# Down products of the second layer: from twenty-four tile products to seven block products

## The chip, the cores and the metric

The kernel runs on one core of one Trainium2 chip. The metric is the device time of one execution in microseconds (us). "TensorE" is the matrix engine (PE in the profile), "VectorE" is DVE, "ScalarE" is ACT, "GpSimd" is POOL; SP only issues DMAs here.

## The reference, cut to what matters

A chunked attention (2 batches, 8 heads, 768 positions, head size 64) gives 1536 tokens of 512 features. Two layers follow, of which only these lines matter:

```python
for e in range(4):                                   # first layer: w1[e] 512x1024, w2[e] 1024x512
    out += p[:, e:e+1] * (np.maximum(x @ w1[e], 0) @ w2[e])
h = x @ w_in                                         # second layer: w_in 512x2048
g = np.where(h > 0, h, np.exp(np.minimum(h, 0)) - 1)
return g @ w_out                                     # w_out 2048x512
```

## The kernel before, in words

**Precision.** Every operand of a product is split into a high and a low part ("hh" and "hl" for the hidden values, "uh"/"ul" and "dh"/"dl" for up and down weights, "xh"/"xl" for the layer's input): a cast on ScalarE makes the high part and a subtraction on VectorE or GpSimd the low one (`split_task`, L245). A product is three matmuls: high by high, low by high, high by low.

**Units.** Both layers are cut into units (u, g): u counts slices of 512 hidden features (8 in the first layer, 4 in the second), g is one of two groups of 768 tokens. `SEQ` lists the 24 units in order; the last eight, from (8, 0) to (11, 1), are the second layer. A unit is one `up` and then one `down`.

**up (L552)** is a Strassen form (Winograd's): hidden features, input features and tokens are each halved, and 7 block products replace 8. `ORDER` is 1, 7, 6, 2, 5, 4, 3; each product comes in two column halves j, so there are 14 steps of 6 matmuls of 128x384. Three pairs of PSUM banks take part: `ba` (products 1 and 2), `bh` (7 and 4), `bb` (6, 5, 3). ScalarE copies product 1 into `bb`, and products 7 and 6 aside into SBUF (`keep`, L580) before the next product accumulates on the same bank; VectorE adds (`plus`, L589). In the second layer each 128x384 result goes through ELU in `activate` (L497): two activations on ScalarE (L522, L523), one operation on VectorE (L528), and then a cast (L533) and a subtraction (L243) that make hh and hl.

**down (L640)** takes six blocks of 128 tokens, each 12 matmuls of 128x512 (4 slices of features by 3) into one bank of a ring of six, 72 matmuls in all, and adds the bank to y in SBUF: ScalarE copies it at u = 8 (L693), VectorE adds at u = 9 to 11 (L695). At u = 11 y goes to DRAM (L697); the last block is done in two halves of 256 columns. y of both groups stays in SBUF.

**Weights.** Up weights come as four blocks per j into `rawp`; `prep_pair` (L283) splits three of them, makes four block sums on GpSimd (L300), and splits those. Down weights of a unit come into `rawd` and are split by `prep_down` (L307). The second layer's weights arrive as 64-bit floats; `convert` (L321) turns them to 32 bits during the first layer and stores them in a DRAM stash.

**Between the layers** the first layer's y is transposed on TensorE by blocks (`flip`, L699), and `combine` (L434) makes the sums of the new input's blocks (4 differences and 4 splits of 128x768) on VectorE or GpSimd as `RANK["engx1"]` says.

**Order.** Nothing is issued in program order. `Plan` collects tasks with an engine, a duration and a rank, and `issue` simulates the engines and issues, on whichever engine can start first, the ready task of least rank. So each engine's queue order is fixed when the kernel is built, and an engine waits at the head of its queue. The offsets in `RANK` and the engines in `BY` are constants.

Of the kernel before, what the change touches and what calls it, by code (L numbers as in the profile page):

```python
# [19 lines left out]
P = 128  # L20
# [4 lines left out]
NB = S // P  # L25
# [20 lines left out]
Q = 2 * P  # L46

# [16 lines left out]
    "probs": 23.52, "a0": 2.68, "a0s": 1.6, "lead": 7.03, "pair": 7.15, "pairs": -2.83, "plead": 4.25, "c0": -100.24,  # L64
# [22 lines left out]


def pick(key, default):
    return BY.get(key, default)  # L90


ORDER = (1, 7, 6, 2, 5, 4, 3)

PLAIN = ((4, 5, 6, 7), (4, 5, 6, 7))


class Plan:

# [77 lines left out]
def kernel(ctx, tc, att, w1, w2, w_in, w_out, probs, out):  # L177
# [374 lines left out]
    def up(u, g, rank):  # L552
# [3 lines left out]
        for n, (p, j) in enumerate([(p, j) for j in range(2) for p in ORDER] if apart else [(p, j) for p in ORDER for j in range(2)]):  # L556
# [54 lines left out]
            elif p == 3:  # L611
                act(j, 1, acc, kb)
# [385 lines left out]
```

## Time and profile before

| | |
|---|---|
| median of 3 runs | 809.6 us (809.51 to 810.88) |
| span of the profiled execution | 808.4 us |
| TensorE busy | 797.4 us (99%) |
| VectorE / ScalarE / GpSimd busy | 513.0 / 422.9 / 264.2 us (63% / 52% / 33%) |
| granted TensorE clock | 0.999 |
| DMA | 72.11 MB, 89 GB/s over the span |

The profiled execution has a span of 808.4 us from its first to its last instruction; its own time outside the profiler is not listed, and the median of the three runs is 1.2 us above that span. Matmul durations overlap, because matmuls are pipelined; the spacing of their starts is what they cost.

### The profile page before, as it was taken

What the parts mean: (1) busy time and instruction counts of PE and PEld (TensorE: products, weight loads), DVE (VectorE), ACT (ScalarE), POOL (GpSimd) and SP (SyncE); (2) the same over time, 40 slices, a digit from 0 to 9 for tenths busy, and PEclk for the clock granted to TensorE, in tenths of its full rate; (3) what the DMA queues carried; (4) which work ended last, traced back from release to release, by engine and by line L of the source; (5) the groups of instructions that cost most, each with busy time, mean ns of one, the idle gap of its engine ahead of it and who ended that gap; (6) DMA issues with size and microseconds to landing.
All of it is one profiled execution on the core that took longest, in us unless ns stands there. A gap on an engine that the chain in (4) does not pass through costs nothing.

```text
span 808.4 us, 12197 instructions
## 1 busy us (share of the span) xinstructions
PE 797.4 (99%) x4684; PEld 720.5 (89%) x4684; DVE 513.0 (63%) x860; ACT 422.9 (52%) x869; POOL 264.2 (33%) x250
## 2 busy tenths in 40 slices
PE   7999999999999999999999999999999999999998
PEld 6888889989989989989989889899898898898997
DVE  5895559985865875865875745745734536537533
ACT  6877635715425425425435336456766555555642
POOL 2447374305124124223322422653214215205202
PEclk9999999999999999999999999999999999999999
DMA  8965013522511511511421300213003003000112
GB/s 313 344 245 170 29 52 118 182 92 68 172 61 66 194 61 59 208 53 67 156 78 66 131 1 1 70 46 94 1 1 105 0 1 105 1 1 1 38 41 78
DMA packets 27418, 72.11 MB, mean 89 GB/s; under 512 B 3168, under 2 KB 3424, under 8 KB 27360
## 3 DMA queue, kind: packets, MB, share of 16 engines
q1 hardware_dynamic: 27360, 71.34, 26.0%
q8 instruction: 36, 0.59, 0.3%
q14 instruction: 22, 0.18, 0.1%
HBM read 59.79 MB, written 11.53 MB: 88 GB/s over the span
## 4 chain that ended last, share of the span: by engine, by line
PE 90%; DVE 3%; ACT 3%; DMA 2%; POOL 1%; issue 1%; SPq 0%; ACTq 0%; DVEq 0%; POOLq 0%
PE bank L662 47%; PE bank L568 39%; DMA qk<-in_att_dram 2%; PE bank L628 1%; DMA area<-in_w_in_dram 1%; POOL rawp L300 1%; PE bank L784 1%; PE bank L861 1%; PE bank L707 1%; ACT e L812 0%; DVE abd L849 0%; ACT abd L849 0%; PE bank L841 0%; DVE ul L243 0%; DVE m L806 0%
## 5 line engine op out<-in xcount | busy, mean ns | idle before, releaser
L662 PE MATMUL bank<-dh,hh 128*128 128x512 f32 x580 | 225.8, 389 | 0.0
L662 PE MATMUL bank<-dh,hl 128*128 128x512 f32 x580 | 225.2, 388 | 0.0
L662 PE MATMUL bank<-dl,hh 128*128 128x512 f32 x580 | 225.1, 388 | 0.0
L568 PE MATMUL bank<-xh,uh 128*128 128x384 f32 x644 | 218.4, 339 | 0.9 <-DVE c L589 0.5
L568 PE MATMUL bank<-xh,ul 128*128 128x384 f32 x644 | 216.8, 337 | 0.0
L568 PE MATMUL bank<-xl,uh 128*128 128x384 f32 x644 | 216.7, 337 | 0.0
L243 POOL TENSOR_TENSOR hl<-c,hh 128x384 fp32r<-128x384 f32 x63 | 69.6, 1117 | 224.8 <-ACT hh L533 221.1
L662 PEld LDWEIGHTS bank<-dh,hl 128*128 128x128 f32 x580 | 108.9, 188 | 23.1 <-DVE hl L508 0.2
L662 PEld LDWEIGHTS bank<-dl,hh 128*128 128x128 f32 x580 | 108.9, 188 | 21.3
L662 PEld LDWEIGHTS bank<-dh,hh 128*128 128x128 f32 x580 | 108.9, 188 | 21.1
L568 PEld LDWEIGHTS bank<-xh,uh 128*128 128x128 f32 x644 | 120.9, 188 | 3.2 <-DVE c L589 1.1
L568 PEld LDWEIGHTS bank<-xl,uh 128*128 128x128 f32 x644 | 120.9, 188 | 0.8
L568 PEld LDWEIGHTS bank<-xh,ul 128*128 128x128 f32 x644 | 120.9, 188 | 0.1
L300 POOL TENSOR_TENSOR rawp<-rawp 128x256 f32<-128x256 f32 x96 | 86.2, 910 | 20.6 <-DVE ul L243 14.4
L688 DVE SCALAR_TENSOR_TENSOR y<-bank,pr,y 128x512 f32<-128x512 f32 x84 | 62.6, 746 | 41.2 <-PE bank L662 41.1
L243 POOL TENSOR_TENSOR hl<-area,hh 128x384 fp32r<-128x384 f32 x32 | 36.7, 1161 | 152.8 <-ACT hh L533 152.1
L243 DVE TENSOR_TENSOR ul<-rawp,uh 128x512 fp32r<-128x512 f32 (+1 forms) x71 | 67.7, 969 | 28.5 <-ACT uh L247 28.4
L247 ACT CAST uh<-rawp 128x512 fp32r<-128x512 f32 (+1 forms) x76 | 51.9, 685 | 60.9 <-POOL rawp L300 59.5
L375 ACT ACTIVATE area<-area 128x512 f32<-128x512 f32 x32 | 20.3, 634 | 82.8 <-DVE area L366 82.7
L528 DVE SCALAR_TENSOR_TENSOR area<-area,bank 128x384 f32<-128x384 f32 x32 | 17.6, 549 | 68.7 <-ACT area L523 68.7
L580 ACT COPY bank<-bank 128x384 f32<-128x384 f32 x46 | 21.2, 463 | 73.7 <-PE bank L568 73.7
L243 POOL TENSOR_TENSOR dl<-rawd,dh 128x512 fp32r<-128x512 f32 x14 | 22.5, 1611 | 66.4 <-ACT dh L247 66.4
(87 smaller groups left out, 953.4 us busy)
## 6 DMA issues: line engine op xcount, KB each, us to landing
rawp<-in_w_dram SPq DMA_DIRECT2D x18, 512.0 KB, 3.3
rawd<-in_w_dram SPq DMA_DIRECT2D x36, 256.0 KB, 3.8
qk<-in_att_dram SPq DMA_DIRECT2D x11, 768.0 KB, 6.3
area<-in_w_in_dram SPq DMA_DIRECT2D x16, 512.0 KB, 3.7
stash<-area SPq DMA_DIRECT2D x32, 256.0 KB, 2.2
area<-in_w_out_dram SPq DMA_DIRECT2D x16, 512.0 KB, 3.7
v<-in_att_dram SPq DMA_DIRECT2D x12, 512.0 KB, 5.3
rawp<-stash SPq DMA_DIRECT2D x16, 256.0 KB, 2.7
```

What stands on the lines that cost most here:

```text
L243: e.tensor_tensor(out=dst, in0=a, in1=b, op=ALU.subtract)
L247: add("A", t_a(n), rank, lambda: A.copy(out=hi(), in_=src), rkeys, hkeys)
L300: lambda o=o, a=a, b=b, op=op: G.tensor_tensor(out=r[:, o], in0=r[:, a], in1=r[:, b], op=op),
L375: lambda: A.activation(out=t, in_=t, func=AF.Copy, scale=2.0**-20, bias=1.0),
L528: lambda: V.scalar_tensor_tensor(out=r, in0=r, scalar=-1.0, in1=v, op0=ALU.add, op1=ALU.max),
L568: PE.matmul(out=acc, lhsT=s[:, k], rhs=x[g][ib][:, k], start=(first and k == 0 and m == 0), stop=(k == 1 and m == 2), skip_group_check=True,)
L580: add("A", t_a(TN), r - 2, lambda: A.copy(out=dst, in_=acc), kb, kd)
L628: PE.matmul(out=acc, lhsT=s[:, k], rhs=x[0][ib][:, k], start=(q == 0 and k == 0 and m == 0), stop=(q == 1 and k == 1 and m == 2),)
L662: PE.matmul(out=po, lhsT=s[f][half][:, t0 : t0 + P], rhs=w[f][:, c], start=(q == 0 and i == 0), stop=(q == NF - 1 and i == 2),)
L688: lambda: V.scalar_tensor_tensor(out=yy(), in0=po, scalar=p, in1=yy(), op0=ALU.mult, op1=ALU.add),
L707: PE.transpose(ft[:, kt], y[g][tb][:, kt * P : (kt + 1) * P], ident)
L784: PE.matmul(out=s4[64 * cp : 64 * cp + 64, hp, ch], lhsT=qbd[:, hp, c], rhs=k[:, hp, c], start=True, stop=True,)
```

## The change

1. The second layer's down product becomes the same seven block products as up: output features, hidden features and tokens halved, the down weights stationary, the hidden values moving (`down2`). It comes out transposed (features on the partitions, tokens along the free axis), and the output in DRAM has that layout; the host turns it round.
2. The hidden values are kept unsplit in "quads" of 128x768. `hidden_diff` makes four differences on VectorE per unit, `hidden_split` seven splits (ScalarE casts; four subtractions on VectorE and three on GpSimd) into four rotating buffers `sh`/`sl`. The eight casts and eight subtractions of 128x384 in `activate` go.
3. The down weights need block sums too. They are made on GpSimd during the first layer (`sums_ahead`, at the places in `ROUNDS`), stored to DRAM and loaded by `prep_pair(kind="d")`; `prep_down` is no longer used in the second layer.
4. The second layer's order is up(8,0), up(8,1), down(8,0), up(9,0), down(8,1), ..., down(11,0), down(11,1). Up and down take turns on the bank pairs: `bh` stays with every run, the other three pairs rotate (`turn_banks`).
5. y of the second layer has one buffer for both groups. After each down it is stored to DRAM in four pieces of 384 KB, and loaded back before the same group's next down. `gather` adds the products to it, in twelve operations of 128x384 per unit (on ScalarE the first six of those at u = 8).
6. Memory: dh/dl, rawd and y become single tiles that the second layer reuses once the first has ended (`switch2`); y of the second group is freed for low parts of the down weights ("late").
7. Ranks change: `pp` 40.18 to 16.59, `fx` -18.99 to 2.61, `x1` 51.82 to 47.43, `engx1` "GGVV" to "VVVV", and new ones for the added tasks. `up` is unchanged but for where its results go.

```diff
+ROUNDS = {6: [(NU1, "d")], 10: [(NU1 + 1, "d")], 12: [(NU1 + 2, "d")], 14: [(NU1 + 3, "d")]}
+SUMS = {s for ss in ROUNDS.values() for s in ss}
...
-    rawd = [t(f"rawd{f}", [CH]) for f in range(NF)]
-    dhi = [t(f"dh{f}", [CH], F32R) for f in range(NF)]
-    dlo = [t(f"dl{f}", [CH], F32R) for f in range(NF)]
-    hh = [[t(f"hh{f}_{n}", [TN], F32R) for n in range(2)] for f in range(NF)]
-    hl = [[t(f"hl{f}_{n}", [TN], F32R) for n in range(2)] for f in range(NF)]
-    y = [[t(f"y0_{tb}", [DM]) for tb in range(NB)]]
+    dmem = t("dmem", [2 * NF * CH], F32R)
+    dhi, dlo = ([dmem[:, (n * NF + f) * CH : (n * NF + f + 1) * CH] for f in range(NF)] for n in range(2))
+    rmem = t("rmem", [NF * CH])
+    rawd = [rmem[:, f * CH : (f + 1) * CH] for f in range(NF)]
+    sh = [t(f"sh{s}", [2, TN], F32R) for s in range(4)]
+    sl = [t(f"sl{s}", [2, TN], F32R) for s in range(4)]
+    hh = [[sh[2 * n + f // 2][:, f % 2] for n in range(2)] for f in range(NF)]
+    hl = [[sl[2 * n + f // 2][:, f % 2] for n in range(2)] for f in range(NF)]
+    ymem = [t("y0", [NB * DM])]
+    y = [[ymem[0][:, tb * DM : (tb + 1) * DM] for tb in range(NB)]]
+    late = []
...
+    def operand(kind, lo, j, i):
+        if kind == "u":
+            return (ulo if lo else uhi)[j][i]
+        o, n = (0, 3, 5)[i], part[i][1]
+        if not lo:
+            m, c = dmem, 7 * j + o
+        elif (j, i) == (0, 2):
+            m, c = dmem, 14
+        else:
+            m, c = late[0], 5 * j + o
+        return m[:, c * Q : (c + n) * Q].rearrange("p (n c) -> p n c", c=Q)
...
+    def prep_pair(u, j, rank, lead, by=None, plain=False, kind="u"):
+        if (u, kind) in SUMS:
+            load_pair(u, j, rank - lead, kind)
+            split_blocks(u, j, 0, rank, *part[0], by=by, kind=kind)
+            add(
+                "D",
+                1.46,
+                rank - lead + 2,
+                lambda: nc.sync.dma_start(out=rawp[j].rearrange("p b c -> p (b c)"), in_=stash[u, kind, "s", j]),
+                [("ss", u, kind, j)],
+                [("rp", j, i) for i in range(4)],
+            )
+        else:
+            load_pair(u, j, rank - lead, kind)
+            split_blocks(u, j, 0, rank, *part[0], by=by, kind=kind)
+            if plain:
+                split_blocks(u, j, 2, rank, 3, 1, 1, by=by)
+                return
+            sums(j, rank)
+        for i in (1, 2):
+            split_blocks(u, j, i, rank + 2, *part[i], by=by, kind=kind)
+    def sums_ahead(u, kind, j, rank):
+        load_pair(u, j, rank - 8, kind)
+        sums(j, rank)
+        def store():
+            stash[u, kind, "s", j] = dram.tile([P, 4 * Q], F32, name=f"sums{u}{kind}{j}")
+            nc.sync.dma_start(out=stash[u, kind, "s", j], in_=rawp[j].rearrange("p b c -> p (b c)"))
+        add("D", 1.46, rank, store, [("rp", j, i) for i in range(4)], [("ss", u, kind, j)])
+    def sums(j, rank):
...
+    def elu(r, kr, v, vkeys, rank):
+        add("A", t_a(TN), rank, lambda: A.activation(out=r(), in_=v, func=AF.Relu, scale=-1.0), vkeys, kr)
+        add("A", t_a(TN), rank, lambda: A.activation(out=r(), in_=r(), func=AF.Exp, scale=-1.0), kr, kr)
...
+                if raw is None:
+                    activate(u, f, half, v, vkeys, r + RANK["ac"], ring["e"])
+                else:
+                    q, kq = raw[2 * half + f // 2]
+                    elu(lambda: q()[:, f % 2], kq[f % 2], v, vkeys, r + RANK["ac"])
...
+    def turn_banks():
+        (ba, bh, bb), fr = ring["up"], ring["free"]
+        ring["up"], ring["free"] = (fr, bh, ba), bb
...
+    def quads():
+        qs = []
+        for i in range(2):
+            qs.append((lambda i=i: rmem[:, i * QT : (i + 1) * QT].rearrange("p (k t) -> p k t", k=2), [[("yx", i, k)] for k in range(2)]))
+        for i in (4, 3, 2, 1, 0):
+            o = i * QT
+            qs.append(
+                (
+                    lambda o=o: area[:, o : o + QT].rearrange("p (k t) -> p k t", k=2),
+                    [grains(o + k * TN, TN) for k in range(2)],
+                )
+            )
+        return qs
+    def flat(q):
+        return q[1][0] + q[1][1]
+    def hidden_diff(eng, o, a, b, rank):
+        e, d = (V, t_v(QT)) if eng == "V" else (G, t_g(QT))
+        add(eng, d, rank, lambda: sub(e, o[0](), a[0](), b[0]()), flat(a) + flat(b), flat(o), port=True)
+    def hidden_split(q, s, rank, eng):
+        keys = [[(k, 2 * (s % 2) + f, s // 2) for f in range(2)] for k in ("hh", "hl")]
+        add("A", t_a(QT), rank, lambda: A.copy(out=sh[s], in_=q[0]()), flat(q), keys[0])
+        e, d = (V, t_v(QT)) if eng == "V" else (G, t_g(QT))
+        add(eng, d, rank, lambda: sub(e, sl[s], q[0](), sh[s].bitcast(F32)), flat(q) + keys[0], keys[1], port=True)
+    def hidden_first(st, rank):
+        a, b, c, d, e = st["q"][:5]
+        s0 = st["slot"] = ring["slot"]
+        ring["slot"] = (s0 + 7) % 4
+        slot = [(s0 + n) % 4 for n in range(7)]
+        eh, ed = RANK["enghs"], RANK["enghd"]
+        hidden_split(a, slot[0], rank + RANK["h0"], eh[0])
+        hidden_diff(ed[0], a, d, a, rank + RANK["hd0"])
+        hidden_diff(ed[1], e, b, a, rank + RANK["hd1"])
+        hidden_diff(ed[2], d, b, d, rank + RANK["hd2"])
+        hidden_split(d, slot[1], rank + RANK["h1"], eh[1])
+        hidden_split(e, slot[2], rank + RANK["h2"], eh[2])
+        hidden_split(c, slot[3], rank + RANK["h3"], eh[3])
+        hidden_diff(ed[3], c, c, e, rank + RANK["hd3"])
+    def down2(i, st, rank):
+        u, g = SEQ[i]
+        a, b, c, d, e = st["q"][:5]
+        slot = [(st["slot"] + n) % 4 for n in range(7)]
+        ba, bh, bb = ring["up"]
+        last = u == NU - 1
+        if u > NU1:
+            for q in range(4):
+                add(
+                    "D",
+                    1.1,
+                    rank + RANK["yl"] + 2 * q,
+                    lambda q=q: nc.sync.dma_start(out=yq[q], in_=stash["y", u - 1, g, q]),
+                    [("ys", u - 1, g, q)],
+                    [("yq", q, k) for k in range(2)],
+                )
+        done = [0] * 4
+        def gather(q, j, acc, kb, r, first, final):
+            v, ky = yq[q][:, j], [("yq", q, j)]
+            if u == NU1 and first:
+                add("A", t_a(TN), r - 2, lambda: A.copy(out=v, in_=acc), kb, ky)
+            else:
+                add("V", T_P, r - 2, lambda: V.tensor_tensor(out=v, in0=acc, in1=v, op=ALU.add), kb + ky, ky)
+            if not final:
+                return
+            if last:
+                add("D", 0.6, r, lambda: nc.sync.dma_start(out=out[g, q // 2, q % 2][:, j], in_=v), ky, ())
+            elif j:
+                def store():
+                    stash["y", u, g, q] = dram.tile([P, 2, TN], F32, name=f"y{u}{g}{q}")
+                    nc.sync.dma_start(out=stash["y", u, g, q], in_=yq[q])
+                add("D", 1.1, r, store, [("yq", q, k) for k in range(2)], [("ys", u, g, q)])
+        for n, p in enumerate(ORDER):
+            if n in (1, 2, 3):
+                x = (a, c, b)[n - 1]
+                hidden_split(x, slot[n + 3], rank + RANK[f"h{n + 3}"], RANK["enghs"][n + 3])
+            ia, _ = PROD[p]
+            ii, k0 = place[ia]
+            s = slot[n]
+            hkeys = [(k, 2 * (s % 2) + f, s // 2) for k in ("hh", "hl") for f in range(2)]
+            for j in range(2):
+                bk = (ba if p in (1, 2) else bh if p in (7, 4) else bb)[j]
+                acc, kb = bank[bk][:, :TN], [("b", bk)]
+                r = rank + 2 * n + j
+                def mm(j=j, ii=ii, k0=k0, s=s, acc=acc, first=p in (1, 7)):
+                    wh, wl = (
+                        operand("d", lo, j, ii)[:, k0].rearrange("p (k c) -> p k c", k=2) for lo in range(2)
+                    )
+                    for k in range(2):
+                        for m, (w, x) in enumerate(((wh, sh), (wh, sl), (wl, sh))):
+                            PE.matmul(
+                                out=acc,
+                                lhsT=w[:, k],
+                                rhs=x[s][:, k],
+                                start=(first and k == 0 and m == 0),
+                                stop=(k == 1 and m == 2),
+                                skip_group_check=True,
+                            )
+                add("PE", 1.051, r, mm, [("dh", j, ii), ("dl", j, ii)] + hkeys, kb)
+                if p == 1:
+                    add(
+                        "A",
+                        t_a(TN),
+                        r - 2,
+                        lambda acc=acc, o=bank[bb[j]][:, :TN]: A.copy(out=o, in_=acc),
+                        kb,
+                        [("b", bb[j])],
+                    )
+                for q, first, final in {
+                    7: [(3, True, False)],
+                    6: [(2, True, False)],
+                    2: [(0, True, True)],
+                    5: [(3, False, True)],
+                    4: [(2, False, True)],
+                    3: [(1, True, True)],
+                }.get(p, ()):
+                    gather(q, j, acc, kb, r, first, final)
...
+        def switch2():
+            gone.close()
+            late.append(t("late", [12 * Q], F32R, ctx.enter_context(tc.tile_pool(name="last", bufs=1))))
...
+            for n, (v, kind) in enumerate(ROUNDS.get(i, ())):
+                for j in range(2):
+                    sums_ahead(v, kind, j, at(i) + RANK["sa"] + RANK["sas"] * (2 * n + j))
+        was = [("dh", f) for f in range(NF)] + [("dl", f) for f in range(NF)] + [("rd", f) for f in range(NF)]
+        was += [("y", g, tb) for g in range(B) for tb in range(NB)]
+        now = [(k, j, i) for k in ("dh", "dl") for j in range(2) for i in range(3)]
+        now += [(k, q, j) for k, n in (("yq", 4), ("yx", 2)) for q in range(n) for j in range(2)]
+        add("N", 0, 480, switch2, was, now)
+        ring["up"], ring["free"] = ((4, 5), (2, 3), (0, 1)), (6, 7)
+        base, step = at(FIRST2), RANK["step"]
+        runs = [("u", FIRST2)]
+        for i in range(FIRST2, len(SEQ)):
+            runs += [("u", i + 1)] if i + 1 < len(SEQ) else []
+            runs += [("d", i)]
+        hidden = quads()
+        state = {}
+        for j in range(2):
+            prep_pair(NU1, j, base + RANK["p2f"] + RANK["p2s"] * j, 8, kind="d")
+        for n, (kind, i) in enumerate(runs):
+            u, g = SEQ[i]
+            rank = base + step * n
+            later = base + step * (n + 3)
+            if kind == "u":
+                st = state[i] = {"q": hidden}
+                x, z = hidden[5:]
+                a, b, c, d, e = hidden[:5]
+                hidden = [d, e, x, z, a, b, c]
+                up(u, g, rank, [a, c, d, b])
+                if n == 0:
+                    hidden_first(st, base + 2 * step)
+            else:
+                down2(i, state[i], rank)
+                if i + 1 < len(SEQ):
+                    hidden_first(state[i + 1], later - step)
+            turn_banks()
+            if g == B - 1 and u + 1 < NU:
+                for j in range(2):
+                    prep_pair(u + 1, j, rank + step + RANK["p2" + kind] + RANK["p2s"] * j, 8, kind=kind)
```

## Rows read from the trace of the kernel before

**Rows 1.** The page: span, then busy time, share and instructions of each engine.

```profile
span 808.4 us, 12197 instructions
...
PE 797.4 (99%) x4684; PEld 720.5 (89%) x4684; DVE 513.0 (63%) x860; ACT 422.9 (52%) x869; POOL 264.2 (33%) x250
```

**Rows 2.** Waits of TensorE, 60 to 808 us: total, times, longest.

```profile
PE bank L568 <- DVE c L589: 0.5, 1, 0.5
PE bank L568 <- ACT p L580: 0.4, 1, 0.4
```

**Rows 3.** The chain that ended last, in order of time: start, us, what.

```profile
571.27 16.36 PE bank L662 x72
587.63 14.84 PE bank L568 x84
602.47 16.32 PE bank L662 x72
618.79 14.58 PE bank L568 x84
...
788.80 16.49 PE bank L662 x84
805.31 0.42 DVE y L695
```

**Rows 4.** Windows: length, busy us of PE, PEld, DVE, ACT, POOL, clock, DMA.

```profile
100.00:200.00 100.00, 100.00 (x500) 90.20 (x499) 76.54 (x117) 49.40 (x93) 44.31 (x37) 1.00 0.31 103
618.79:680.90 62.11, 62.11 (x314) 56.40 (x313) 32.05 (x53) 34.89 (x71) 16.99 (x17) 1.00 0.10 30
300.00:540.00 240.00, 240.00 (x1224) 218.52 (x1223) 156.07 (x253) 110.49 (x218) 77.03 (x71) 1.00 0.24 79
```

**Rows 5.** Groups by form, VectorE, 618.79 to 680.90 us: busy, mean ns, idle.

```profile
L243 DVE TENSOR_TENSOR dl<-rawd,dh 128x512 fp32r<-128x512 f32 x4 | 2.6, 685 | 0.0
```

**Rows 6.** The same for ScalarE.

```profile
L533 ACT CAST hh<-area 128x384 fp32r<-128x384 f32 x16 | 7.7, 508 | 0.8 <-DVE area L528 0.6
...
L247 ACT CAST uh<-rawp 128x768 fp32r<-128x768 f32 x2 | 1.6, 819 | 0.0
```

**Rows 7.** Timeline of VectorE, 545 to 612 us: start, us, instruction, idle before.

```profile
566.58 0.95 DVE L243 TENSOR_TENSOR area<-area 128x768 f32<-128x768 f32 x1
567.45 0.55 DVE L589 TENSOR_TENSOR c<-bank,p 128x384 f32<-128x384 f32 x1
567.91 0.55 DVE L243 TENSOR_TENSOR hl<-area,hh 128x384 fp32r<-128x384 f32 x1
...
577.53 3.87 DVE L243 TENSOR_TENSOR xl<-area,xh 128x768 fp32r<-128x768 f32 x3
```

**Rows 8.** Timeline of VectorE, 105 to 114 us.

```profile
105.81 2.60 DVE L243 TENSOR_TENSOR area<-area 128x768 f32<-128x768 f32 x1 [0.74 <-POOL area L243]
```

**Rows 9.** Timeline of GpSimd, 103 to 114 us.

```profile
105.74 1.85 POOL L243 TENSOR_TENSOR xl<-area,xh 128x768 fp32r<-128x768 f32 x1
```

**Rows 10.** Timeline of VectorE, 603 to 611 us.

```profile
605.95 0.97 DVE L243 TENSOR_TENSOR hl<-area,hh 128x384 fp32r<-128x384 f32 x1 [1.84 <-ACT hh L533]
606.84 0.54 DVE L528 SCALAR_TENSOR_TENSOR area<-area,bank 128x384 f32<-128x384 f32 x1
```

**Rows 11.** Timeline of GpSimd, 603 to 611 us.

```profile
604.95 3.58 POOL L300 TENSOR_TENSOR rawp<-rawp 128x256 f32<-128x256 f32 x4
```

**Rows 12.** The page: the costliest groups, the block sums on GpSimd.

```profile
L300 POOL TENSOR_TENSOR rawp<-rawp 128x256 f32<-128x256 f32 x96 | 86.2, 910 | 20.6 <-DVE ul L243 14.4
```

**Rows 13.** The page: DMA issues, KB each, us from issue to landing.

```profile
stash<-area SPq DMA_DIRECT2D x32, 256.0 KB, 2.2
...
rawp<-stash SPq DMA_DIRECT2D x16, 256.0 KB, 2.7
```

**Rows 14.** DMA issues of the output, the same columns.

```profile
out_dram<-y SPq DMA_DIRECT2D x11, 256.0 KB, 2.0
...
out_dram<-y SPq DMA_DIRECT2D x2, 128.0 KB, 1.7
```

More of the change, by code (lines that the diff above doesn't have):

```diff
@@ L46 @@
 Q = 2 * P
+QT = 2 * TN
+FIRST2 = SEQ.index((NU1, 0))
 A11, A12, A22, S2, S4, S1, S3 = range(7)
@@ L227 @@
     xf = [area[:, n * KT * TN : (n + 1) * KT * TN].rearrange("p (k t) -> p k t", k=KT) for n in range(2)]
-    eluv = [2 * KT * TN + i * TN for i in range(3)]
     stash = {}
+    yq = [ymem[0][:, q * QT : (q + 1) * QT].rearrange("p (k t) -> p k t", k=2) for q in range(4)]
     def load_probs(rank):
@@ L249, in split_task, with load_pair @@
         add(eng, d, rank, lambda: sub(e, lo(), src, hi().bitcast(F32)), rkeys + hkeys, lkeys, port=rkeys[0][0] != "b")
-    def load_pair(u, j, rank):
+    def load_pair(u, j, rank, kind="u"):
         keys = [("rp", j, i) for i in range(4)]
@@ L261, in load_pair, with split_blocks @@
                 lambda i=i: nc.sync.dma_start(
-                    out=rawp[j][:, 2 * i : 2 * i + 2].rearrange("p b c -> p (b c)"), in_=stash[u, "u", 2 * j + i]
+                    out=rawp[j][:, 2 * i : 2 * i + 2].rearrange("p b c -> p (b c)"), in_=stash[u, kind, 2 * j + i]
                 ),
-                [("st", u, "u", 2 * j + i)],
+                [("st", u, kind, 2 * j + i)],
                 keys[2 * i : 2 * i + 2],
             )
-    def split_blocks(u, j, i, rank, o, n, to=0, by=None):
+    def operand(kind, lo, j, i):
[9 more added lines that the diff above has]
+        return m[:, c * Q : (c + n) * Q].rearrange("p (n c) -> p n c", c=Q)
+    def split_blocks(u, j, i, rank, o, n, to=0, by=None, kind="u"):
         keys = [("rp", j, k) for k in range(o, o + n)]
@@ L303, in prep_pair @@
             )
-        for i in (1, 2):
-            split_blocks(u, j, i, rank + 2, *part[i], by=by)
     def prep_down(u, f, rank, lead, eng, by=None):
@@ L495, in scratch @@
         return cbuf[c], [("c", c)]
+    def elu(r, kr, v, vkeys, rank):
+        add("A", t_a(TN), rank, lambda: A.activation(out=r(), in_=v, func=AF.Relu, scale=-1.0), vkeys, kr)
+        add("A", t_a(TN), rank, lambda: A.activation(out=r(), in_=r(), func=AF.Exp, scale=-1.0), kr, kr)
+        add(
+            "V",
+            T_P,
+            rank + 1,
+            lambda: V.scalar_tensor_tensor(out=r(), in0=r(), scalar=-1.0, in1=v, op0=ALU.add, op1=ALU.max),
+            kr + vkeys,
+            kr,
+            port=vkeys[0][0] != "b",
+        )
     def activate(u, f, half, v, vkeys, rank, n, short=False):
@@ L501, in activate @@
         kh, kl = ("hh", f, half), ("hl", f, half)
-        if u < NU1 and (short or not half):
+        if short or not half:
             add("A", t_a(TN), rank, lambda: A.activation(out=h, in_=v, func=AF.Relu), vkeys, [kh])
@@ L550, in flip_bank, with up @@
         return ring["flips"][ring["m"] % 2]
-    def up(u, g, rank):
+    def up(u, g, rank, raw=None):
         ba, bh, bb = ring["up"]
@@ L647, in down, with down_block @@
                 r = late + 2.63 * (tb - TN // P)
-            last = (u, g, tb) == (NU - 1, B - 1, NB - 1)
-            for c in (slice(0, Q), slice(Q, DM)) if last else (slice(0, DM),):
-                down_block(u, g, tb, c, r, i in FIRST)
+            down_block(u, g, tb, r, i in FIRST)
             if i in LAST1:
                 flip(g, tb, r + 6)
-    def down_block(u, g, tb, c, r, first):
-        n = c.stop - c.start
+    def down_block(u, g, tb, r, first):
         b = next_bank()
-        po, kb = bank[b][:, :n], [("b", b)]
+        po, kb = bank[b], [("b", b)]
         half, t0 = divmod(tb * P, TN)
@@ L893, in switch @@
             xl.append([t(f"xl1_{o}", [2, TN], F32R, top) for o in range(7)])
-            y.append([t(f"y1_{tb}", [DM], F32, top) for tb in range(NB)])
+            ymem.append(t("y1", [NB * DM], F32, gone.enter_context(tc.tile_pool(name="gone", bufs=1))))
+            y.append([ymem[1][:, tb * DM : (tb + 1) * DM] for tb in range(NB)])
+        def switch2():
+            gone.close()
+            late.append(t("late", [12 * Q], F32R, ctx.enter_context(tc.tile_pool(name="last", bufs=1))))
         def at(i):
@@ L929 @@
             convert(i, RANK["conv"] + RANK["convs"] * i)
-        for i, (u, g) in enumerate(SEQ):
+        for i, (u, g) in enumerate(SEQ[:FIRST2]):
             if i:
```

80 lines of the change are left out of this document (28 added, 52 removed), and 39 rows, old and new, of tables (BY, RANK).

## The prediction

> **What bounds the kernel now.** I read the page first. TensorE is busy for 797.4 of 808.4 us, the next engine, VectorE, for 63% [rows 1]. A busy share alone doesn't prove a bound, so the waits of TensorE come next: from 60 us to the end it waited twice for another engine in the chain of the two layers, 0.5 and 0.4 us [rows 2]. Third, the chain that ended last: in the second layer it is nothing but ups and downs end to end [rows 3]. So time is the number of matmuls by the spacing of their starts, and an edit that takes columns from TensorE is worth what it takes, as long as nobody makes TensorE wait. The granted clock is 1.00, which is the 2.4 GHz level [rows 4], and the change leaves TensorE no planned pause that could lower it.
>
> **What the products cost.** A down of 72 matmuls of 128x512 takes 16.32 to 16.36 us, that is 227 ns a matmul. An up of 84 matmuls of 128x384 takes 14.84 us for one group of tokens and 14.58 for the other, 177 and 174 ns [rows 3]. The new down is 84 matmuls of the up's shape. There is no row for it with weights and moving data where they will lie, so I bound it by these two: 14.58 and 14.84. The eight downs take 130.9 us now (seven by 16.34, and 16.49 for the last with its halves); they would take 116.6 to 118.7. The gain is 12.2 to 14.3 us; I take the middle, **13.2**.
>
> **The end.** Now the last VectorE operation starts at 805.31 and takes 0.42 us [rows 3]; a DMA of 128 KB follows, 1.7 us [rows 14]. Then it will be an operation of 128x384, 0.55 us [rows 7], and 192 KB, between 1.7 and 2.0 us [rows 14]. **+0.3**. The last two downs follow each other without an up between them, and the one y buffer has to be sent out and loaded again in that time: for the piece of product 6 the final addition comes after the sixth product of the first down (12.5 us into it), 2.0 us out, some 3 us in, so at 18 us; TensorE needs its addition done before product 5 of the second down, at 14.7 + 8.4 = 23.1 us. Five us of cover hide it at no cost; without them the cost is what the pieces are late.
>
> **The other y traffic and the stores of sums** are covered likewise. A store of 256 KB lands after 2.2 us, a load after 2.7 [rows 13]; a 384 KB piece is a little slower, say 7 us for both. Between two downs lies an up of 14.7 us. On SP's queue the loads stand behind stores that wait for `gather`, all within the same 14.7 us. Cost nothing; with that cover gone, a few us for each down.
>
> **What moves to the vector engines.** I count for one weight index, two units of each kind, and price each operation by the spacing of starts: 0.47 us for 384 columns, 0.87 for 768 [rows 7], 0.61 for 512 (0.685 less the 0.08 overlap that the other two show) [rows 5].
> VectorE: 48 operations of 384 (8 `plus`, 16 ELU, 24 `gather`) 22.6 us; 20 of 768 (8 differences, 8 splits, 4 weight splits) 17.4; 8 weight splits of 512 4.9. Sum 44.9 us, against 32.1 busy now [rows 4].
> GpSimd: 6 splits of 768 at 1.85 [rows 9], 11.1, and 8 block sums at 0.91 [rows 12], 7.3. Sum 18.4, against 17.0.
> ScalarE: 34.9 now [rows 4], less 16 casts at 0.51, plus 14 at 0.82 [rows 6] and 4 copies of product 1 at about 0.5; the weight casts nearly cancel. Some 40.
> TensorE's time for the same work falls from 62.1 to about 58.8 us. So VectorE goes from 52% to 76%, ScalarE to 69%, GpSimd to 31%. None reaches TensorE's time, if VectorE and GpSimd can run side by side.
>
> **Do they?** At 105.81 us a VectorE difference of 128x768 takes 2.60 us [rows 8] where 0.95 is usual [rows 7]; a GpSimd operation from 105.74 holds until 107.59 [rows 9], and 0.82 us after that the difference is done. At 605.95 a subtraction takes 0.97 beside GpSimd's sums, but the ELU operation that reads a bank still takes 0.54 [rows 10, 11]. So operations of two SBUF inputs wait for GpSimd, those that read a bank don't. The Trainium skill states this as a rule in "SBUF — State Buffer", section "SBUF: two separate sides": the pair of ports is a lock held for a whole instruction, and a VectorE operation with two SBUF inputs is blocked against a GpSimd operation that reads SBUF. The trace agrees, by the 2.60 and the 0.54; that rule taken without any overlap is the third rival below.
> By rows: if VectorE waited for all of GpSimd's time, a weight index would take 44.9 + 18.4 = 63.3 us, over 58.8; with none of it, 44.9. Against the worst case: 40 of VectorE's 48 short operations read a bank, 18.8 us of cover for 18.4 of GpSimd. And from 100 to 200 us VectorE and GpSimd were busy 76.5 and 44.3 us, 121% together, while TensorE was busy for 100.00 [rows 4]. The layer ahead comes to 63.3 in 58.8, 108%. I take stalls near nothing for throughput.
>
> **A new deadline.** In an up the bank of product 6 must be read before product 5 adds to it, three products or 3.1 us later, and ScalarE does that (`keep`). In the new down VectorE does it (`gather`), except at u = 8, and VectorE is the fuller engine. `gather` has a low rank, so it should wait for one operation at most: 0.87 us as a rule, 2.60 when GpSimd holds the ports. 2.60 + 0.55 is 3.15 us, just at the deadline, with the handover between engines on top. Behind a late `gather` stand products 5 and 3 on that bank, and then the next up. Bounds: nothing, or 2.6 us for each of six downs (two blocked operations ahead of it). I take 0.17 each, **+1.0**.
>
> **The step between the layers.** up(8,1) now starts when up(8,0) ends, at about 571.3 instead of 587.6 [rows 3]. Its second product needs a split of `combine` by 573.4. Before, the last three splits ended at 581.4 [rows 7], and with that order TensorE would wait some 5 us. Now VectorE alone does the differences and can begin when the last transposed block is copied, about 562: four differences and two splits are 5.2 us and the ELU of up(8,0) 5.6, which gives 572.8. Then down(8,0) at 586.1 needs the ELU, the differences, two splits and the first weight splits: combine 7.0, ELU 5.6, hidden 5.2, weights 1.7, and some 2.8 of up(8,1)'s ELU (five operations), 22.3 us in 24. Close. Bounds 0 and 5; nearest to 0, since each sum fits: **+1.0**.
>
> **The first layer** gets 32 block sums, 29.1 us of GpSimd [rows 12], within about 300 to 540 us. VectorE and GpSimd were busy 156 and 77 of 240 us there [rows 4]; with 29 more it is 109%, under the 121% that cost nothing. The changed ranks reorder its queues; the waits there are 0.9 us in all [rows 2], so it can gain that, or lose as much. I take 0.
>
> **Sum**, on the profiled span: 808.4 - 13.2 + 0.3 + 1.0 + 1.0 = 797.5 us; the median of the runs stands 1.2 us above the span, so **798.7 us**.
>
> **Rivals.**
> *Late at the step, 0.16.* The splits for up(8,1) or the hidden values for down(8,0) come 4 to 8 us late instead of 1. For: two sums within 2 us of their room. Against: both fit, and only VectorE must. Time 802 to 806.5.
> *The gather deadline, 0.10, the side of slower.* VectorE's queue holds two blocked operations ahead of product 6's `gather` in the downs from u = 9 on: 2.6 us by six is 15.6 in place of 1.0, which gives 813.3. It turns the change into a loss once a down waits more than 13 us over six, 2.2 us. For: 2.60 us was seen. Against: one blocked operation alone costs next to nothing, and between such waits VectorE idles a quarter of the time.
> *VectorE and GpSimd in series, 0.05.* Four weight indices at 63.3 are 253.2, less the first index's up weights, made earlier (4.2 on VectorE, 7.3 on GpSimd), plus `combine` (7.0): 248.7 us. TensorE's second layer takes 130.9 + 4 x 29.42 = 248.6 now. So 808.4 + 0.1 + 0.3 + 1.2 = 810.0, no change: the matmuls go and nothing is gained. For: the blocked rows. Against: 121% from 100 to 200 us, though a blocked operation counts as busy, so that this overstates the overlap.
> *More than forecast, 0.05*: the smallest down, no stall, and the 0.9 us of waits gone: 795.5 or below.
>
> **Chances.** The forecast has 0.64, with its own range 795.5 to 802. The range to hold 8 in 10 adds the first rival: 795.5 to 806.5. A measurement of this kernel can tell about 0.2%, 1.6 us, from no change. Faster is the forecast, the late step, the larger gain and a little of the series case: 0.86; within 0.2% the rest of the series case, 0.03; slower the deadline and the other edge of the series case, 0.11.
>
> **What would show it.** In the chain of waits the second layer should alternate pieces of 84 matmuls of 14.6 to 14.8 us, sixteen of them; pieces of 15 us or more for the down say that the matmul price was wrong. VectorE should be busy some 45 to 55 us in a stretch of 58.8, GpSimd 17 to 19. TensorE's waits by line should name no engine for more than 2 us in all; a wait of the first product of a down for a split, or one for combine's differences near 573 us, is the late step; waits of product 5 for VectorE in each down are the deadline. The prediction is wrong if TensorE's busy share falls under 97% after 560 us.

## The result, and the profile after

The changed kernel takes 799.89 us (median of 4 runs, 799.42 to 801.97), the kernel before beside it 810.24: a ratio of 0.9875, 95% interval 0.9857 to 0.9892. Measured twice more beside the experiments below it gave 0.9876 (0.9860 to 0.9893) and 0.9884 (0.9869 to 0.9898). The prediction was 798.7 us, range 795.5 to 806.5, faster.

The page of the profiled execution, span and engines, to be read beside [rows 1]:

```profile
span 797.6 us, 12744 instructions
...
PE 784.6 (98%) x4768; PEld 729.4 (91%) x4768; DVE 598.5 (75%) x952; ACT 445.0 (56%) x893; POOL 304.6 (38%) x269
...
DMA packets 39949, 104.65 MB, mean 131 GB/s; under 512 B 4560, under 2 KB 6608, under 8 KB 39888
```

TensorE is still the engine that fills the span; VectorE went from 63% to 75%, and the DMA bytes from 72 to 105 MB. The chain that ended last, in the second layer, beside [rows 3] (start, us, what):

```profile
560.02 26.08 PE bank L620 x150
586.10 12.70 PE bank L775 x72
598.80 2.08 PE bank L620 x12
600.88 2.12 PE bank L775 x12
603.00 12.48 PE bank L620 x72
...
663.71 12.50 PE bank L620 x72
676.21 14.80 PE bank L775 x84
691.01 14.56 PE bank L620 x84
...
764.29 29.82 PE bank L775 x168
794.13 0.56 DVE y L743
```

L620 is an up, L775 a new down, L743 `gather`. A down is 14.80 us, in place of 16.32 to 16.36. Between 624.99 and 662.40 us, left out above, this chain leaves TensorE and runs through VectorE, loads, ScalarE and GpSimd; the two waits below lie there. The first two ups run through without a break (150 matmuls from 560.02 to 586.10), so the step between the layers costs nothing here. The order also lets two steps of the next up in before the last two steps of a down (598.80). Waits of TensorE, 556 to 797 us (total, times, longest), beside [rows 2]:

```profile
PE bank L775 <- DVE y L743: 0.8, 1, 0.8
PE bank L775 <- ACT bank L790: 0.6, 1, 0.6
```

**Where the 10.8 us of span went** (808.4 to 797.6). The first layer ends as before: the down that started at 506.10 starts at 506.60, and up(8,0) ends some 0.2 us later. Eight downs went from 130.9 to 118.4 us, -12.5. The four ups of the second group went from 14.84 to 14.56 us (up(8,1) to about 14.6); with 0.06 us from the three later ups of the first group that is -1.1, which I had not forecast. From there to the last matmul the pieces add up to 220.4 us (118.4 + 14.62 + 6 x 14.56) and the trace takes 222.6 (571.5 to 794.1): 2.2 us of waits and restarts. The end is 0.4 longer (0.56 for 0.42 in the last operation, 2.9 for 2.7 behind it). 0.2 - 12.5 - 1.1 + 2.2 + 0.4 = -10.8.

Windows of the second layer, about one up and one down each (length, busy us of PE, PEld, DVE, ACT, POOL, and then clock, DMA share and GB/s), beside [rows 4]:

```profile
615.50:644.80 29.30, 29.30 (x169) 29.30 (x169) 20.69 (x29) 22.20 (x44) 6.13 (x3) 1.00 0.54 181
644.80:674.10 29.30, 27.84 (x158) 27.20 (x157) 23.81 (x36) 18.34 (x36) 13.23 (x11) 1.00 0.43 144
674.10:703.40 29.30, 29.30 (x170) 29.30 (x169) 25.72 (x41) 20.29 (x39) 6.62 (x3) 1.00 0.49 166
703.40:732.70 29.30, 29.30 (x170) 29.30 (x169) 24.61 (x38) 19.14 (x37) 13.16 (x11) 1.00 0.46 158
```

For each weight index (two windows, 58.6 us) VectorE is busy 44.5 and 50.3 us, GpSimd 19.4 and 19.8, ScalarE 40.5 and 39.4. The granted clock stays at 1.00, the 2.4 GHz level.

**The two waits.** Timeline of VectorE, 652 to 664 us (start, us, instruction, idle before):

```profile
653.95 2.02 DVE L259 TENSOR_TENSOR ul<-rawp,uh 128x768 fp32r<-128x768 f32 x1
...
657.29 2.01 DVE L259 TENSOR_TENSOR ul<-rawp,uh 128x512 fp32r<-128x512 f32 x2
660.58 1.29 DVE L259 TENSOR_TENSOR ul<-rawp,uh 128x512 fp32r<-128x512 f32 x2 [1.28 <-ACT uh L263]
661.79 1.95 DVE L743 TENSOR_TENSOR y<-bank,y 128x384 f32<-128x384 f32 x4
```

`gather` (661.79) stands in the queue behind a split of an up weight, and that waits 1.28 us for ScalarE's cast, which waited for GpSimd's block sums. It is the addition of product 5, and TensorE's last step of that down, product 3 on the same bank, starts 0.84 us late, at 662.40. Timeline of ScalarE, 640 to 652 us:

```profile
643.95 0.83 ACT L263 CAST uh<-rawp 128x768 fp32r<-128x768 f32 x1 [1.15 <-DMA rawp<-stash]
...
647.92 0.48 ACT L790 COPY bank<-bank 128x384 f32<-128x384 f32 x1
...
650.21 0.48 ACT L790 COPY bank<-bank 128x384 f32<-128x384 f32 x1
```

ScalarE stands for 1.15 us at the head of its queue for an up weight; ELU of the up before and the two copies of product 1 (L790) are behind it, and TensorE waits 0.6 us for the second, at 650.21. Timeline of SP, 610 to 670 us, where L731 loads y, L752 stores it, L320 and L277 load weights:

```profile
629.13 1.65 SPq L320 DMA_DIRECT2D rawp<-sums9d  x2
630.84 0.90 SPq L752 DMA_DIRECT2D y<-y  x2
631.83 6.01 SPq L731 DMA_DIRECT2D y<-y  x3
637.95 1.79 SPq L277 DMA_DIRECT2D rawp<-stash  x4
```

Three pieces of y are issued ahead of that weight, and the loads of this size issued between 620 and 650 us land after 5.5 us (median), where one landed after 2.7 us before [rows 13]. DMA issues in that stretch:

```profile
rawp<-stash SPq DMA_DIRECT2D x4, 256.0 KB, 5.5
```

### The profile page after: what moved, and what is told of

The parts are those of the page before. It is cut to its first block, busy times and chain, and to the rows that moved or that the text cites. A ratio compares the mean times of both kernels' runs of the same rounds, so it can differ in the third digit from the quotient of the medians.

```text
span 797.6 us, 12744 instructions
## 1 busy us (share of the span) xinstructions
PE 784.6 (98%) x4768; PEld 729.4 (91%) x4768; DVE 598.5 (75%) x952; ACT 445.0 (56%) x893; POOL 304.6 (38%) x269
## 4 chain that ended last, share of the span: by engine, by line
PE 84%; DMA 4%; DVE 4%; ACT 3%; POOL 2%; issue 2%; SPq 0%; POOLq 0%; DVEq 0%; ACTq 0%
PE bank L620 37%; PE bank L849 31%; PE bank L775 13%; DMA qk<-in_att_dram 2%; POOL rawp L356 2%; PE bank L818 1%; PE bank L1040 1%; DMA rawp<-stash 1%; DMA area<-in_w_in_dram 1%; PE bank L886 1%; DMA rawp<-sums9d 1%; ACT abd L1028 1%; PE bank L963 1%; DVE ul L259 1%; ACT e L991 0%
## 5 line engine op out<-in xcount | busy, mean ns | idle before, releaser
L849 PE MATMUL bank<-dmem,sh 128*128 128x512 f32 x768 | 237.7, 391 | 0.0
L620 PE MATMUL bank<-xh,uh 128*128 128x384 f32 x644 | 217.9, 338 | 0.9 <-DVE c L641 0.5
L620 PE MATMUL bank<-xh,ul 128*128 128x384 f32 x644 | 216.4, 336 | 0.0
L620 PE MATMUL bank<-xl,uh 128*128 128x384 f32 x644 | 216.4, 336 | 0.0
L849 PEld LDWEIGHTS bank<-dmem,sh 128*128 128x128 f32 x768 | 143.2, 188 | 28.3
L849 PE MATMUL bank<-dmem,sl 128*128 128x512 f32 x384 | 149.8, 390 | 0.0
L259 POOL TENSOR_TENSOR sl<-c,sh 128x384 fp32r<-128x384 f32 x63 | 68.2, 1090 | 211.2 <-ACT sh L585 208.6
L356 POOL TENSOR_TENSOR rawp<-rawp 128x256 f32<-128x256 f32 x128 | 121.9, 964 | 47.5 <-DVE ul L259 31.6
L620 PEld LDWEIGHTS bank<-xh,uh 128*128 128x128 f32 x644 | 120.9, 188 | 2.4 <-DVE c L641 0.8
L620 PEld LDWEIGHTS bank<-xl,uh 128*128 128x128 f32 x644 | 120.9, 188 | 0.7
L620 PEld LDWEIGHTS bank<-xh,ul 128*128 128x128 f32 x644 | 120.9, 188 | 0.0
L871 DVE SCALAR_TENSOR_TENSOR y<-bank,pr,y 128x512 f32<-128x512 f32 x84 | 62.6, 746 | 44.6 <-PE bank L849 44.5
L849 PEld LDWEIGHTS bank<-dmem,sl 128*128 128x128 f32 x384 | 72.1, 188 | 15.4 <-DVE sl L575 0.2
L775 PE MATMUL bank<-sh,dmem 128*128 128x384 f32 x256 | 81.9, 340 | 1.5 <-DVE y L743 0.8
L775 PE MATMUL bank<-sl,dmem 128*128 128x384 f32 x224 | 75.3, 336 | 0.0
L775 PE MATMUL bank<-sh,late 128*128 128x384 f32 x192 | 64.9, 338 | 0.0
L775 PEld LDWEIGHTS bank<-sh,dmem 128*128 128x128 f32 x256 | 47.6, 188 | 2.1 <-DVE y L743 1.2
L743 DVE TENSOR_TENSOR y<-bank,y 128x384 f32<-128x384 f32 x80 | 41.2, 549 | 7.2 <-PE bank L775 7.0
```

Of the source, the lines that this page charges most:

```text
L259: e.tensor_tensor(out=dst, in0=a, in1=b, op=ALU.subtract)
L356: lambda o=o, a=a, b=b, op=op: G.tensor_tensor(out=r[:, o], in0=r[:, a], in1=r[:, b], op=op),
L620: PE.matmul(out=acc, lhsT=s[:, k], rhs=x[g][ib][:, k], start=(first and k == 0 and m == 0), stop=(k == 1 and m == 2), skip_group_check=True,)
L743: add("V", T_P, r - 2, lambda: V.tensor_tensor(out=v, in0=acc, in1=v, op=ALU.add), kb + ky, ky)
L775: PE.matmul(out=acc, lhsT=w[:, k], rhs=x[s][:, k], start=(first and k == 0 and m == 0), stop=(k == 1 and m == 2), skip_group_check=True,)
L849: PE.matmul(out=po, lhsT=s[f][half][:, t0 : t0 + P], rhs=w[f], start=(q == 0 and i == 0), stop=(q == NF - 1 and i == 2),)
```

## The experiments

Three theories. **A**: the gain is the matmuls' time alone; the other engines and the DMAs have room, and what is lost is a wait at the head of an in-order queue here or there. **B**: VectorE with GpSimd, in series because of the ports, is already the bound. **C**: the order (one up ahead) and the y traffic don't matter. The experiments ran in groups of four, four, three and one, in the order below; the kernels of a group share a chip and the runs of the kernel before.

**One up ahead undone.**

```diff
-            runs += [("u", i + 1)] if i + 1 < len(SEQ) else []
             runs += [("d", i)]
+            runs += [("u", i + 1)] if i + 1 < len(SEQ) else []
```

(`hidden_first` is then called after each up.)

> The second layer's order is up, down, up, down again, everything else as in the changed kernel. Theory (the down needs the last result of its up, so one up of cover is what makes the block form possible without waits): the second product of each down needs a difference of the quad that the up's last product fills; after the last matmul come 0.48 + 0.52 + 0.55 us of ELU, a difference 0.95, a cast 0.82 and a low part 0.95 to 1.85, 4.3 to 5.2 us, with other work of the queues in front up to 8, less the 2.1 us of the first product: 2 to 6 us of wait in each of 8 downs, 816 to 848 us, slower than the kernel before. Rival (the products' order hides it): 799 to 803 us.

Measured: 843.69 us (one run), before 810.55. Waits of TensorE, 556 to 842 us, then windows with the granted clock (the next to last three columns are POOL, PEclk, DMA share):

```profile
PE bank L775 <- DVE sl L259: 10.3, 11, 1.7
PE bank L775 <- POOL sl L259: 9.1, 8, 1.9
PE bank L775 <- ACT sh L698: 6.5, 8, 1.3
```

```profile
606.00:612.00 6.00, 3.77 (x18) 3.03 (x17) 5.32 (x8) 5.57 (x11) 3.21 (x4) 0.90 0.00 0
612.00:620.00 8.00, 7.32 (x34) 6.68 (x33) 8.00 (x6) 5.08 (x9) 6.11 (x3) 0.86 0.26 98
```

25.9 us of waits for the hidden values' parts, as expected; and around waits of about 2 us TensorE runs partly at the 1.2 GHz level. The span is 44 us longer (841.9 for 797.6). The granted clock from 560 us to the end was 0.96 on the mean, which by my estimate is worth at most 11 us (0.04 of 282); the other 7 us are not accounted for. In this order the block form is slower than the kernel before by 33 us, with queue offsets that had been set for the other order, so a part of the 33 may be theirs. C falls for the order.

**y not sent to DRAM.** `if u > NU1:` before the loads and `elif j:` before the stores become false.

> The stores and loads of the second layer's y between units are left out (both groups add into the one buffer, so y isn't the reference's). Theory (48 transfers of 384 KB lie under the ups): no change, 799 to 801 us. Rival (they hold up SP's queue, and by it the weights that VectorE waited for at 660 us): 1 to 2 us faster, 797.5 to 798.9 us.

Measured: 798.94 us, ratio 0.9857 (0.9842 to 0.9872). The wait for L790 is gone, 0.6 us for L743 stays, and ScalarE waits for no up weight any more between 628 and 652 us. The time lies between the two expectations, and the interval overlaps that of the changed kernel, so it doesn't decide; the wait that went is the rival's, and by it the y traffic isn't quite hidden.

**Block sums of the down weights in the second layer.** `ROUNDS = {}`.

> The block sums of the down weights are made in the second layer, not ahead. GpSimd gets 8 more sums of 0.8 to 0.9 us for each of 4 weight indices, 7.3 us in 58.8. Theory (VectorE has room, but a weight split that waits for sums on GpSimd holds VectorE's queue and so a gather): waits of 0.5 to 2 us for each weight index, 801 to 808 us. Rival 1 (VectorE and GpSimd work in series and are the bound): 7.3 x 4 = 29 us more, about 829 us. Rival 2 (all hidden): 799 to 801 us.

Measured: 808.07 us, ratio 0.9967 (0.9955 to 0.9978): 8 us of the 10 are gone, by about 29 us of GpSimd's time (32 sums). The two largest waits of TensorE, 550 us to the end, of 5.6 us in all:

```profile
PE bank L775 <- DVE y L743: 3.0, 3, 1.3
PE bank L620 <- ACT bank L632: 1.2, 3, 0.5
```

As theory A expected, at its upper end; B's 829 did not come.

**`combine` as before**, `"x1": 51.82`, `"engx1": "GGVV"`.

> The sums of the second group's input go back to two differences on GpSimd and two on VectorE with the old rank, all else as in the changed kernel. Theory (at the step between the layers up(8,1) has 16 us less room, so combine must be early): its second product waits 2 to 6 us at about 573 us, 802 to 806 us. Rival (the order adapts and the room suffices): 799 to 801 us.

Measured: 802.78 us, ratio 0.9902 (0.9880 to 0.9924). In its trace the stretch from up(8,0)'s last long piece to up(9,0)'s takes 44.7 us (starts 561.63 to 606.29), 1.6 more than in the changed kernel (559.77 to 602.84); the second layer after it is the same. Of the 3.6 us by which its profiled run is longer, 1.5 us stand already at 100 us, long before the step. The sign is as expected, the 1.6 us are under the 2 to 6, and no single wait of TensorE over 0.9 us stands there.

**The changed kernel again, and with more work on VectorE.**

> The changed kernel itself, run beside the next three on one chip, so that differences of 1 us can be told. Every theory: 799 to 801 us, 0.986 to 0.989 of the kernel before.

Measured: 801.13 us, ratio 0.9876. Its waits for L790 are 1.7 us in this run.

```diff
         add(eng, d, rank, lambda: sub(e, o[0](), a[0](), b[0]()), ...)
+        add(eng, d, rank, lambda: e.tensor_tensor(out=o[0](), in0=o[0](), in1=o[0](), op=ALU.max), flat(o), flat(o), port=True)
```

> After each of the four differences of a unit VectorE does one more operation of 128x768 with two SBUF inputs (a maximum of the quad with itself, which changes no value): 0.87 us x 4 = 3.5 us more for each of 8 units, 28 us in all. VectorE was busy 24.5 us in a stretch of 29.3 and would be at 28. Theory (VectorE has 4 to 5 us of room in 29.3, no more): 0 to 1 us for each unit, mostly as late gathers, 801 to 808 us. Rival (VectorE with GpSimd is already the bound): all 28 us, about 828 us.

Measured: 811.32 us, ratio 1.0007 (0.9997 to 1.0018), 10 us over the changed kernel beside it. 28 us of added work cost 10, so VectorE was not the bound, against B; but the room was smaller than A had it, since 10 is more than the 1 to 8 expected. The waits are spread: six kinds from 0.6 to 1.7 us, for a low part, a `gather`, a `keep`. The added operations also lengthen the path from a difference to its split, and how much of the 10 us comes by that was not tried.

**Sums of the up weights ahead too**, for u = 9, and for all.

```diff
-ROUNDS = {6: [(NU1, "d")], 10: [(NU1 + 1, "d")], 12: ..., 14: ...}
+ROUNDS = {6: [(NU1, "d")], 8: [(NU1 + 1, "u")], 10: [(NU1 + 1, "d")], 12: ..., 14: ...}
+# e8 also: 11: [(NU1 + 2, "u")], 13: [(NU1 + 3, "u")]
```

> The block sums of one up weight index of the second layer (u = 9) are made in the first layer too. Theory (the longest wait of the second layer, 0.8 us at 662 us, is a gather behind weight splits whose sums GpSimd is late with; that is the weight index after, so this one alone moves the work before it): 0 to 0.8 us faster than the changed kernel, 799 to 800 us. Rival (GpSimd's and SP's queues in the first layer have no more room): 1 us or more slower.

> The same for u = 9, 10 and 11, so that no block sum is left in the second layer. Theory: the wait of 0.8 us goes, and GpSimd has only the low parts; 0.5 to 1.5 us faster than the changed kernel, 798.4 to 799.4 us. Rival (24 more sums and 6 more stores in the first layer delay its weights): 1 to 5 us slower than the changed kernel.

Measured: 800.29 us, ratio 0.9874 (0.9856 to 0.9893), and 801.86, ratio 0.9886 (0.9870 to 0.9902): no gain that can be told. In the second the wait for L743 is gone, as expected, and the first layer shows no new wait; but the wait for L790 is 1.5 us, with ScalarE 1.9 us at a weight that lands late. The larger of the two causes was untouched. Nor does this trace show what the wait for L743 came from: the unedited kernel measured beside the next experiment has none either, though VectorE stands the same 1.28 us for the same cast there. Both traces have 1.5 us of waits for L790, and a lowered clock behind them, so that TensorE is late itself. The unedited kernel's window (length, busy us of PE, PEld, DVE, ACT, POOL, clock, DMA share, GB/s):

```profile
652.00:657.00 5.00, 4.57 (x17) 4.57 (x18) 4.96 (x7) 3.01 (x6) 1.50 (x2) 0.66 0.00 0
```

**y loaded after the weights.**

```diff
-                    [("ys", u - 1, g, q)],
+                    [("ys", u - 1, g, q)] + ([("dl", 1, 1)] if g == 0 else []),
```

> The changed kernel itself, beside the next two on one chip. Every theory: 799 to 802 us.

> The first group's y is loaded back only after the block sums of the down weights have been split, so that on SP's queue the next up weights go ahead of most of y's pieces; nothing else changes. Theory (the waits of 1.4 to 2.6 us near 645 us come from ScalarE, which stands at the head of its queue for an up weight that lands 5.5 us after its issue behind y's pieces, with ELU and the copy of product 1 behind it): the wait for that copy goes, 0.5 to 2 us faster than the changed kernel beside it, 798 to 800 us. Rival (y's pieces then come late for the additions): 1 to 5 us slower. Rival 2 (the waits had another cause): no difference.

Measured: the changed kernel 800.97 us, ratio 0.9884; this one 799.85, ratio 0.9868 (0.9853 to 0.9882). The intervals overlap, so the time doesn't settle it; the traces do. Timeline of SP, 626 to 650 us, DMA issues of 620 to 650 us, and all waits of TensorE after 540 us:

```profile
635.73 2.58 SPq L277 DMA_DIRECT2D rawp<-stash  x2
638.40 0.38 SPq L731 DMA_DIRECT2D y<-y  x1
638.89 0.84 SPq L277 DMA_DIRECT2D rawp<-stash  x2
639.82 1.34 SPq L731 DMA_DIRECT2D y<-y  x3
```

```profile
y<-y SPq DMA_DIRECT2D x8, 384.0 KB, 5.7
...
rawp<-stash SPq DMA_DIRECT2D x4, 256.0 KB, 3.4
```

```profile
PE bank L775 <- DVE y L743: 0.7, 1, 0.7
```

Most weights go first, some 2 us earlier, and land after 3.4 us in place of 5.5; y's pieces land after 5.7 in place of 4.3, and come in time. The wait for L790 is gone, as it is without the y traffic, while all three traces of the changed kernel have it (0.6, 1.7, 1.5 us).

**All low parts on GpSimd**, `"enghs": "GGGGGGG"`.

> All seven low parts of the hidden values of a unit are made by GpSimd instead of three: GpSimd gets 4 x 1.85 = 7.4 us more for each unit, VectorE 4 x 0.87 = 3.5 us less. Theory (VectorE's operations with two SBUF inputs wait while GpSimd runs): VectorE loses more room than it gains, 1 to 6 us slower than the changed kernel, 801 to 807 us. Rival (the two run side by side, and only VectorE's own work counts): equal or faster, 798 to 801 us.

Measured: 809.69 us, ratio 0.9990 (0.9979 to 1.0002): 8.7 us over the changed kernel, more than expected, and not by the way expected. VectorE was busy 177 us after 556 us, in place of 197. Timeline of ScalarE, then of GpSimd, then windows with the clock:

```profile
665.15 1.31 ACT L263 CAST uh<-rawp 128x512 fp32r<-128x512 f32 x2 [4.44 <-POOL rawp L356]
...
667.10 0.47 ACT L632 COPY bank<-bank 128x384 f32<-128x384 f32 x1
```

```profile
656.80 1.84 POOL L259 TENSOR_TENSOR sl<-rmem,sh 128x768 fp32r<-128x768 f32 x1
658.61 1.45 POOL L356 TENSOR_TENSOR rawp<-rawp 128x256 f32<-128x256 f32 x1
660.02 1.85 POOL L259 TENSOR_TENSOR sl<-area,sh 128x768 fp32r<-128x768 f32 x1
661.84 6.04 POOL L356 TENSOR_TENSOR rawp<-rawp 128x256 f32<-128x256 f32 x6
```

```profile
662.00:668.00 6.00, 3.31 (x18) 3.00 (x17) 2.52 (x3) 2.44 (x5) 5.84 (x7) 0.91 0.40 120
668.00:674.00 6.00, 6.00 (x21) 6.00 (x21) 5.44 (x8) 1.39 (x3) 1.66 (x1) 0.53 0.70 234
```

Low parts and block sums take turns on GpSimd, the up weights' sums end late, ScalarE waits 4.44 us for one at the head of its queue, and TensorE 2.7 us for the copy behind it; then TensorE runs 6 us at the 1.2 GHz level. The largest wait is again behind a queue's head. How much the ports add to the lateness of the sums was not separated.

**Both edits together**: all sums of the up weights ahead, and y loaded after the weights.

> The edits of e8 and e10 together: no block sum is left in the second layer, and the first group's y is loaded after the weights. Theory (the two waits of the second layer's steady part have these two causes, and nothing else is late there): no wait over 0.5 us after 600 us, 798.8 to 799.9 us, 0.9855 to 0.987 of the kernel before, the same as e10 or up to 0.8 us faster. Rival (the sums made ahead cost the first layer what they save): 800 to 802 us.

Measured: 798.91 us (797.98 to 799.52), ratio 0.9857 (0.9839 to 0.9876), the lowest ratio of the kernels here, beside that without the y traffic. In its trace TensorE waits for nobody that the profile can name from 540 us to the end, and the chain that ended last is TensorE's alone from 589.84 to 792.71 us. Two of its pieces, where the changed kernel's chain left TensorE:

```profile
645.45 14.79 PE bank L775 x84
660.23 14.56 PE bank L620 x84
```

This settles the cause of the wait for L743 too. VectorE before that `gather`, with y after the weights alone, and then with both edits:

```profile
660.04 1.29 DVE L259 TENSOR_TENSOR ul<-rawp,uh 128x512 fp32r<-128x512 f32 x2 [1.28 <-ACT uh L263]
```

```profile
654.66 2.56 DVE L259 TENSOR_TENSOR ul<-rawp,uh 128x512 fp32r<-128x512 f32 x4
```

The first still has 0.7 us of TensorE waiting for L743; with the sums made ahead VectorE doesn't stand at the split, and the wait is gone, both at a clock of 1.00. So with both edits nothing is left to wait for in the steady second layer. What they are worth together is 1 to 2 us by the medians; the interval still overlaps the changed kernel's.

## Why the prediction was right, step by step

- **Matmul price.** 12.2 to 14.3 us were bounded, 13.2 taken, 12.5 measured: the new down has nearly the dearer of the two spacings (14.80 us, 176 ns). The gain stands or falls with it; the ups add 1.1 and waits take some back.
- **The ups** were taken as unchanged; the second group's fell by 0.28 us each, 1.1 in all. That term was missing.
- **The end**: +0.3 taken, +0.4 measured.
- **Room on the vector engines**: VectorE 45 to 55 us, GpSimd 17 to 19, ScalarE 40 in 58.8 were forecast; 44.5 and 50.3, 19.4 and 19.8, 40.5 and 39.4 came. At u = 8 ScalarE makes eight of a down's twelve additions as copies (16 in two downs), not the six that the list of changes names. With the added operations and with the sums moved back, about a third of the added time came through (10 of 28 us, 8 of 29), so "stalls near nothing" holds for the kernel as it is, and the series rival does not: it needs all of the time.
- **The gather deadline**: of the 1.0 us taken, 0.8 came, but not where it was put. The deadline of product 6 was met; the wait is one addition further on, where product 3 needs the bank that product 5's `gather` reads. The cause taken was an operation lengthened by the ports; what stands in front of the `gather` is a weight split that waits 1.28 us at VectorE's head, and with the sums made ahead that wait went. The ports are not excluded behind it: the split at 653.95 took 2.02 us, where 0.95 is usual for its size, and GpSimd's sums were late.
- **y traffic "cost nothing"** was off by a little: no piece of y came late, but y's pieces make the weights late behind which ScalarE stands, 0.6 to 1.7 us of TensorE's time in three traces. In one of them the clock fell to 0.66 for 5 us behind it, against "no planned pause that could lower it"; this costs more than the wait itself shows. The trace read above is that of the fastest of its four runs. I had asked whether y would be in time, and not what stands behind y on SP's queue.
- **The step between the layers**: +1.0 taken, none seen. Undoing the earlier `combine` costs 1.6 us there in the trace, so the edit was enough and worth about that; the 5 us that bounded it did not come.
- **The first layer**: 0 taken; it ends within 0.5 us of before with 32 more block sums on GpSimd (121.9 us for all of them, 86.2 before).
- **One up ahead** was priced at nothing because the up covers the hidden values; taking that cover away cost 44 us in one run, four times the gain.
- **The signs named ahead**: TensorE was busy 232.6 of the 237.6 us after 560, 97.9%, over the 97% set as the sign of being wrong. The clean row of sixteen pieces did not come: the first downs are interleaved, and the chain left TensorE at the two waits.

The sum came out 0.1 us from the span (797.5 for 797.6) by luck, because the errors cancel: 0.7 less from the matmuls and 0.5 more in waits, the end and the first layer (2.8 for 2.3) against 1.1 from the ups. The step from span to median was mis-sized: 1.2 us were added, and each of the four runs stands 1.8 us above its own span (799.42 over 797.6), so 798.7 is 1.2 us under the 799.89.

## What to carry to other kernels

Where one engine fills the span, a change that takes columns from it is worth the spacing of its matmuls, read from the nearest run of the same shape, provided that a whole stage of other work covers the longer path to its operands. The losses then sit at heads of in-order queues: for each operation that waits on a load or on a slow engine, ask what stands behind it, and put transfers that have time to spare behind the ones that somebody waits for. The other engines' shares, all under 90%, did not show these waits; a timeline of 10 us around one did.

## What I had not expected of the hardware

- The up of the second group, on the same operands, spaces its matmuls by 176.7 ns (14.84 us) nearly everywhere in the first layer of both kernels and in the second layer of the kernel before, and by 173.3 ns (14.56) in the new second layer; the new downs stand at 176. Three ups of the runs here lie between, at 14.68 to 14.69 us. The pairs of banks that an up writes rotate in the new second layer, and its neighbours differ; neither was tried alone, and the cause stays open.
- TensorE's clock fell behind waits in some traces and not in others, and their size alone doesn't tell which. Behind two waits for L790 of at most 1.0 us each it was 0.66 from 652 to 657 us in the third measurement of the changed kernel; in the second it stayed at 1.00 behind two such waits, 1.7 us together. With more work on VectorE it stayed at 1.00 around a wait of 1.7 us. With all low parts on GpSimd it stood at 0.53 for the 6 us after a wait of 2.7 us, and the 72 matmuls of the rest of that up took 15.5 us for 12.5, so that stall cost about twice what its wait shows. With one up ahead undone it fell around most of the downs' waits of about 2 us, but not around the last, where TensorE was busy 2.12 of 4 us:

```profile
824.00:828.00 4.00, 2.12 (x13) 1.80 (x12) 4.00 (x5) 1.59 (x2) 3.16 (x2) 1.00 0.26 94
```
